# Attention in units of 256 tokens by 4 heads: q and k loaded as token pairs, scores as products of 32 rows

## The chip, the core and the metric

The kernel runs on one core of one Trainium2 chip. A core has five engines with a queue of instructions each: TensorE (PE in the profile; the loads of its stationary operand are shown as PEld), VectorE (DVE), ScalarE (ACT), GpSimd (POOL) and SyncE (SP), which here only issues DMAs. Sixteen DMA engines move data between HBM and the on-chip memory SBUF. TensorE writes its results to PSUM, which has 128 partitions and eight banks of 512 float32 values per partition. The metric is the device time of one execution in microseconds (us); lower is better.

## The reference

Inputs are q, k and v of shape 8 x 8 x 576 x 64 (batch, heads, tokens, head width) and two weight matrices, `w_in` (512 x 2048) and `w_out` (2048 x 512), all float32. What is computed, cut to its core:

```python
# attention within chunks of 64 tokens, 9 chunks per batch and head
scores = q_c @ k_c.T / 8
attn = exp(scores - max(scores)); attn /= sum(attn) + 1e-9
out = attn @ v_c
x = out.transpose(0, 2, 1, 3).reshape(4608, 512)   # 8 heads side by side
h = x @ w_in
g = softplus(h)
return g @ w_out                                   # 4608 x 512
```

## The kernel before

**The matrix products.** The 4608 rows of x are treated in nine groups of 512. Each group needs a first product with `w_in` (lines 632 to 642, and line 777 for the six last groups, which are taken in pairs and use a scheme with seven products in place of eight), a softplus, and a second product with `w_out` (line 831). Both run in the format fp32r; each value is split into a high and a low part, so each product consists of three terms. Almost all of TensorE's time goes into these.

**The attention.** A block is 128 rows of x: two chunks of 64 tokens, all 8 heads. There are 36 blocks, four per group of rows. The first four blocks are computed at the start, with TensorE doing the transposes (lines 384 to 450): `pe_t` transposes q and k through PSUM, `pe_tq` and `pe_tk` copy them out on ScalarE, `pe_s` makes the scores, `pe_e` transposes the exponentials, `pe_v` multiplies by v. The other 32 blocks (lines 470 to 609) are worked off between the matrix products: VectorE transposes q and k in 32 x 32 squares (`blk_t`), `blk_s` makes the scores on TensorE, VectorE takes the maximum and subtracts it, ScalarE the exponential, and after the division VectorE transposes the exponentials (`blk_e4`; for four blocks `blk_swap` with DMAs), and `blk_v` multiplies by v.

On TensorE `blk_s` and `blk_v` of two blocks stand together in what the code calls a burst (line 624): v of one pair of blocks and scores of the next pair, in the order v, scores, v, scores. A product there is float32, 64 x 64 x 64, and takes one of four quarters of the array (two halves of the rows by two halves of the columns). `blk_s` and `blk_v` issue 16 such products per block; `pe_s` also 16, but on two quarters alone. There are 17 bursts: the first has scores only, the last v only.

**The loads.** For 32 x 32 transposes on VectorE to turn a 64 x 64 piece into its transpose, its four squares must already lie in exchanged places. For most blocks eight DMAs of 32 KB per tensor put them there (lines 479 to 489), each row of a square being a packet of 128 bytes. Blocks 4, 5 and 9 (`WHOLE`) and the first four are loaded in one or two DMAs with packets of 256 bytes (one token, one head); for blocks 4, 5 and 9 VectorE then moves the squares with four extra transposes of 32 partitions (`blk_t4`). v comes in four DMAs per block.

**The order.** All engines' instructions are written out by a planner (class `Plan`): each task has an engine, an assumed cost, its needs, an urgency and the buffers that it takes. The planner runs through its own clock and emits the tasks in the order in which they would start; so each engine's queue has a fixed order, and an instruction that waits holds up all behind it on its engine. The sequence of the matrix products and bursts on TensorE is fixed by a list (`seq`). The tiles `pa` (two of two PSUM banks each) hold the first product's results, and those of the bursts; the tiles `po` (four of one bank) hold the second product's.

Of the kernel before, what the change touches and what calls it, by code (L numbers as in the profile page):

```python
# [33 lines left out]
class Plan:  # L34
# [10 lines left out]
    HOLD_FROM = 120.0  # L45

# [4 lines left out]
    def add(  # L51
        self, name, eng, cost, fn, needs=(), urg=0.0, table=None, take=(), kb=0, slack=0.0, after=(), port=False, parts=1,
        late={}, room={}
    ):
        self.tasks[name] = dict(
            name=name, eng=eng, cost=cost, fn=fn, needs=list(needs) + list(after), after=set(after), urg=urg, table=table,
            take=take, kb=kb, slack=slack, seq=len(self.tasks), port=port or eng == "POOL", parts=parts, late=late, room=room,
        )
# [97 lines left out]
def chunked_attention_softplus_ffn(  # L156
# [9 lines left out]
    nc = tc.nc  # L166
# [3 lines left out]
    C = 64  # L170
# [172 lines left out]
    def hd(t):  # L343
        return t.rearrange("p (h d) -> p h d", d=D)

    def rows_of(i):
        b, c = divmod(2 * i, NCH)
        if c + 1 < NCH:
            return [(0, P, b, c * C)]
        return [(0, C, b, c * C), (C, C, b + 1, 0)]  # L350

    def pe_load(eng, i, src, n):
        dst = hd(slot(i, n))
        for p0, rows, b, s0 in rows_of(i):
            eng.dma_start(  # L355
                dst[p0 : p0 + rows], src[b, :, s0 : s0 + rows, :].rearrange("h s d -> s h d")
            )
# [3 lines left out]

    def v_load(i, t):
        dv = t.rearrange("p (j c d) -> p j c d", c=2, d=D)
        for c2 in range(2):
            b, c = divmod(2 * i + c2, NCH)
            for a in range(2):
                loader("v", i).dma_start(
                    dv[a * C : (a + 1) * C, :, c2, :],
                    v[b, a * HP : (a + 1) * HP, c * C : (c + 1) * C, :].rearrange("h s d -> s h d"),
                )  # L370
        live["v", i] = t.rearrange("p (j d) -> p j d", d=D)
# [12 lines left out]
    def pe_t(i):  # L384
        if i < 2:
            tq, tk = (po_tile(n) for n in range(2))
        else:
            pa = pa_tile()
            tq, tk = pa[:, 0, :], pa[:, 1, :]
        keep_warm(tq)  # L390
        for dst, n in ((tq, 0), (tk, 1)):
            src = hd(slot(i, n))
            for hp in range(HP):
                nc.tensor.transpose(
                    dst[:, hp * P : (hp + 1) * P], src[:, 2 * hp : 2 * hp + 2, :], ident
                )
        live["t", i] = tq, tk

    def pe_tq(i):
        nc.scalar.copy(slot(i, 3), live["t", i][0])  # L400

    def pe_tk(i):
        copy = nc.scalar.copy if i not in TK else nc.vector.tensor_copy
        copy(slot(i, 4), live["t", i][1])

    def pe_s(i):
        qT, kT = (slot(i, n).rearrange("p (a t) -> p a t", a=HP) for n in (3, 4))
        sc = po_tile(2 + i % 2)
        keep_warm(sc)
        for hp in range(HP):  # L410
            for c2 in range(2):
                for h2 in range(2):
                    r = slice(h2 * C, (h2 + 1) * C)
                    t = slice(c2 * C, (c2 + 1) * C)
                    col = (2 * hp + c2) * C
                    nc.tensor.matmul(
                        sc[r, col : col + C], qT[r, hp, t], kT[r, hp, t], start=hp + c2 == 0, stop=True,
                        skip_group_check=True,
                    )
        live["sc", i] = sc.rearrange("p (a c k) -> p a c k", c=2, k=C)  # L420
        live["e", i] = slot(i, 0).rearrange("p (a c k) -> p a c k", c=2, k=C)

    def pe_e(i):
        tp = po_tile(i)
        keep_warm(tp)
        for hp in range(HP):
            nc.tensor.transpose(tp[:, hp * P : (hp + 1) * P], live["e", i][:, hp], ident)
        live["et", i] = tp
# [4 lines left out]
    def pe_v(i):  # L433
        eT, vt = slot(i, 1).rearrange("p (a t) -> p a t", a=HP), hd(slot(i, 2))
        pa = pa_tile()
        xp = [pa[:, 0, :], pa[:, 1, :]]
        keep_warm(xp[0])
        for hp in range(HP):
            for h2 in range(2):
                for c2 in range(2):  # L440
                    o = slice(((h2 + c2) % 2) * C, ((h2 + c2) % 2 + 1) * C)
                    r = slice(c2 * C, (c2 + 1) * C)
                    nc.tensor.matmul(
                        xp[c2][o, hp * C : (hp + 1) * C],
                        vt[r, 2 * hp + (h2 + c2) % 2, :],
                        eT[r, hp, o],
                        start=True,
                        stop=True,
                    )
        live["xp", i] = pa[:, :, : HP * C].rearrange("p c (a t) -> p c a t", t=C)  # L450
# [19 lines left out]
    def blk_load(i, name, src):  # L470
        dst = home(name, i)
        live[name, i] = dst
        if i in WHOLE:
            for p0, rows, b, s0 in rows_of(i):
                loader(name, i).dma_start(
# [869 lines left out]
```

## Time and profile before

| | |
|---|---|
| time, median of 3 runs | 833.47 us (832.66 to 834.87) |
| the profiled execution's own time | 831.63 us |
| its span, first to last instruction | 829.2 us |
| TensorE busy | 817.2 us, 99% |
| VectorE, ScalarE, GpSimd busy | 487.7, 381.5, 327.0 us |
| DMA packets | 189512, of which 152704 under 512 bytes |
| granted TensorE clock | 0.999 |

The page says how long each engine was busy. "PE" counts the time in which a product was under way, so it hides the small steps between products, and the start of the next piece must be compared with the start of the one before. A float32 product leaves two records, so 16 products show as x32. In a timeline row the columns are start, duration, engine, line, operation, output and inputs, shape, count, and in square brackets how long the engine had been idle before and what ended that. The chain of waits goes back from the last instruction to whatever released each step.

### The profile page before, as it was taken

The page shows a single profiled execution, that of the slowest core. Times are in us where ns is not written, and L with a number is a line of the kernel's source. Part 1 is how long each engine was busy: PE and PEld are TensorE (multiplying, and loading weights), DVE is VectorE, ACT ScalarE, POOL GpSimd, SP SyncE. Part 2 cuts the span into 40 slices and gives each one's busy share as a digit, 9 for nine tenths or more (in the row PEclk, how much of TensorE's full clock was granted, in tenths as well). Part 3 has the DMA queues.
Part 4 walks back from the last instruction along what each step waited for, and adds up shares of the span by engine and source line. Part 5 has one row for each costly group of instructions (what it writes and reads, how often), then busy time and mean ns, then how long its engine had stood idle before and what let it go on. Part 6 is the DMA issues. An engine that isn't in the chain of part 4 may idle for free.

```text
span 829.2 us, 15241 instructions
## 1 busy us (share of the span) xinstructions
PE 817.2 (99%) x5745; PEld 671.5 (81%) x5745; DVE 487.7 (59%) x769; ACT 381.5 (46%) x612; POOL 327.0 (39%) x380
## 2 busy tenths in 40 slices
PE   9899999999999999999999999999999999999998
PEld 7787888888888888888887878888888888888886
DVE  3988985367556587374677786573866632232322
ACT  4867765444534473353543543443444343333322
POOL 1655569686987753212224411222230021321100
PEclk9999999999999999999999999999999999999999
DMA  9987757754475446876576427678362165354322
GB/s 205 268 215 178 212 153 225 218 151 113 84 188 127 115 151 205 211 211 173 161 221 179 127 104 230 172 199 229 120 215 78 51 219 175 117 187 153 102 102 76
DMA packets 189512, 137.33 MB, mean 166 GB/s; under 512 B 152704, under 2 KB 166272, under 8 KB 186496
## 3 DMA queue, kind: packets, MB, share of 16 engines
q1 hardware_dynamic: 178400, 86.68, 38.6%
q0 software_dynamic: 10896, 49.56, 19.4%
q8 instruction: 45, 0.74, 0.4%
q14 instruction: 27, 0.22, 0.1%
q10 hardware_dynamic: 144, 0.13, 0.0%
HBM read 100.14 MB, written 35.13 MB: 163 GB/s over the span
## 4 chain that ended last, share of the span: by engine, by line
PE 91%; DMA 3%; SPq 2%; DVE 2%; ACT 1%; issue 0%; POOL 0%; DVEq 0%; POOLq 0%
PE po L831 46%; PE pa L777 27%; PE pa L641 14%; PE pa L605 2%; SPq L355 2%; PE pa L517 2%; DMA raw<-in_moe_w_out_dram 1%; DMA q<-in_q_dram 1%; DMA raw<-in_moe_w_in_dram 1%; DVE wib L767 0%; SPq L269 0%; DVE mx L562 0%; DMA out_dram<-raw 0%; POOL wib L328 0%; DVE wib L328 0%
## 5 line engine op out<-in xcount | busy, mean ns | idle before, releaser
L796 POOL TENSOR_TENSOR wib<-wib 128x512 f32<-128x512 f32 x48 | 63.5, 1323 | 275.6 <-ACT wib L783 273.7
L831 PE MATMUL po<-late,g_hi 128*128 128x512 f32 x538 | 165.8, 391 | 0.0
L657 DVE TENSOR_TENSOR g_lo<-ends,g_hi 128x512 fp32r<-128x512 f32 x96 | 66.3, 691 | 98.3 <-ACT g_hi L653 94.7
L831 PEld LDWEIGHTS po<-late,g_hi 128*128 128x128 f32 x538 | 100.3, 188 | 21.3 <-DVE late L328 0.3
L777 PE MATMUL pa<-wi_hi,xb 128*128 128x512 f32 x368 | 113.3, 389 | 0.0
L653 ACT CAST g_hi<-ends 128x512 fp32r<-128x512 f32 x96 | 59.3, 618 | 114.7 <-PE po L831 111.3
L831 PE MATMUL po<-wo_hi,g_hi 128*128 128x512 f32 x288 | 109.7, 393 | 0.0
L831 PE MATMUL po<-wo_lo,g_hi 128*128 128x512 f32 x288 | 108.7, 390 | 0.6 <-POOL wo_lo L328 0.6
L831 PE MATMUL po<-late,g_lo 128*128 128x512 f32 x287 | 108.0, 390 | 0.7 <-issue 0.7
L831 PE MATMUL po<-wo_hi,g_lo 128*128 128x512 f32 x288 | 108.5, 389 | 0.0
L777 PE MATMUL pa<-wib,xb 128*128 128x512 f32 x432 | 104.2, 394 | 0.7 <-DVE wib L767 0.7
L777 PEld LDWEIGHTS pa<-wib,xb 128*128 128x128 f32 x432 | 79.2, 188 | 21.8 <-ACT wib L783 5.4
L796 DVE TENSOR_TENSOR wib<-wib,pa 128x512 f32<-128x512 f32 x72 | 49.6, 689 | 66.1 <-PE pa L777 51.4
L777 PEld LDWEIGHTS pa<-wi_hi,xb 128*128 128x128 f32 x368 | 69.0, 188 | 14.4
L777 PE MATMUL pa<-wi_lo,xb 128*128 128x512 f32 x184 | 71.6, 389 | 0.0
L649 ACT ACTIVATE u<-pa 128x512 f32<-128x512 f32 (+1 forms) x50 | 29.1, 581 | 89.0 <-PE pa L641 85.9
L783 ACT COPY wib<-pa 128x512 f32<-128x512 f32 x72 | 39.9, 589 | 62.3 <-PE pa L777 62.3
L804 ACT ACTIVATE ends<-pa 128x512 f32<-128x512 f32 x48 | 28.7, 599 | 80.5 <-PE pa L777 55.7
L831 PEld LDWEIGHTS po<-late,g_lo 128*128 128x128 f32 x287 | 53.9, 188 | 12.4 <-issue 1.1
L831 PEld LDWEIGHTS po<-wo_lo,g_hi 128*128 128x128 f32 x288 | 54.0, 188 | 12.1 <-POOL wo_lo L328 1.1
L831 PEld LDWEIGHTS po<-wo_hi,g_lo 128*128 128x128 f32 x288 | 54.1, 188 | 11.3
L831 PEld LDWEIGHTS po<-wo_hi,g_hi 128*128 128x128 f32 x288 | 53.7, 188 | 11.5 <-POOL wo_hi L324 0.2
(189 smaller groups left out, 1368.9 us busy)
## 6 DMA issues: line engine op xcount, KB each, us to landing
xb<-scratch POOLq DMA_DIRECT2D x23, 1024.0 KB, 5.6
xb<-scratch POOLq DMA_DIRECT2D x24, 768.0 KB, 7.4
spill<-ends SPq DMA_DIRECT2D x21, 512.0 KB, 6.8
ends<-spill SPq DMA_DIRECT2D x21, 512.0 KB, 3.3
out_dram<-raw SPq DMA_DIRECT2D x35, 256.0 KB, 2.8
raw<-in_moe_w_in_dram SPq DMA_DIRECT2D x16, 512.0 KB, 5.6
raw<-in_moe_w_out_dram SPq DMA_DIRECT2D x16, 512.0 KB, 4.4
scratch<-ends SPq DMA_DIRECT2D x16, 512.0 KB, 3.2
```

Of the source, the lines that this page charges most:

```text
L355: eng.dma_start(dst[p0 : p0 + rows], src[b, :, s0 : s0 + rows, :].rearrange("h s d -> s h d"))
L517: nc.tensor.matmul(pa[o, c2, col : col + C], qT[r, a * HP + hl, :], kT[r, a * HP + hl, :], start=True, stop=True,)
L605: nc.tensor.matmul(pa[o, a, col : col + C], vt[r, 4 * j + 2 * h2 + c2, :], eT[r, :, 4 * c2 + 2 * j + h2, :], start=True, stop=True,)
L641: nc.tensor.matmul(ph, wt[:, c, :], x[:, ts_, c, :], start=(n == 0), stop=(n == 3 * KC - 1))
L649: nc.scalar.activation(w["u"], w["ph"], AF.Softplus)
L653: nc.scalar.copy(w["hi"], w["u"])
L657: (nc.gpsimd if pool else nc.vector).tensor_tensor(w["lo"], w["u"], w["hi"].bitcast(F32), op=ALU.subtract)
L777: nc.tensor.matmul(w["bank"][BANK[k]], wts[:, q, c, :], x[:, c, :], start=k < NX and c + n == 0, stop=c == 1 and n == 2, skip_group_check= ...
L783: nc.scalar.copy(tmp_of(n), w["bank"][n])
L796: (nc.gpsimd if what in MIX_POOL else nc.vector).tensor_tensor(out, a, b, op=op)
L804: nc.scalar.activation(u_tiles(j)[i], src, AF.Softplus)
L831: nc.tensor.matmul(pos[w["m"]][t], terms[n][0][:, j * P : (j + 1) * P], terms[n][1], start=(w["first"] and n == 0), stop=n == 2 and (w["la ...
```

## The change

The unit of the attention becomes 256 tokens (four chunks) by 4 heads, in place of 128 tokens by 8 heads. It still has 128 partitions by 512 values, and there are still 36, four for each group of 512 rows.

- **Loads of q and k.** A partition gets a pair of tokens of a chunk, 2 x 64 values that lie side by side in HBM, so a packet has 512 bytes. A unit is one DMA, or two where it reaches into the next batch. v keeps packets of 256 bytes and comes in two DMAs (three at some batch ends).
- **The turn.** One VectorE transpose of 32 x 32 squares (`qk_turn`) now leaves the head width in two halves of 32, each on the 32 partitions of its chunk. It serves the first four units too, where TensorE's transposes and ScalarE's copies (`pe_t`, `pe_tq`, `pe_tk`) go, and takes the place of the extra transposes of `blk_t4`.
- **The scores.** As the head width now lies in two halves on the same 32 partitions, a score is a sum of two products of 32 rows (`a` = 0 and 1): 32 products per unit, on spots of 32 rows by 64 columns of the array; four spots are used, one for each chunk. The second operand is read in steps: its tokens lie as all first ones of the pairs and then all second ones, and reading alternates between the two (distance 32 values). The transposed exponentials are read in the same alternating way in `pe_v` (distance 32 values) and `blk_v` (distance 256 values).
- **The first four units** take their score tiles from `pa` in place of `po`, and `pe_sub` is issued once per bank.
- **The planner** gets new costs for the tasks above (also for `blk_e4`, which has the same instructions as before). The cost of a burst is as it was. A table `SHIFT` of corrections to urgencies is added and left empty.

The diff, cut to what bears on the order and the engines:

```diff
+    def unit(src, i, first, count):
+        at = i // 2 * 4 + first
+        b, c = divmod(at, NCH)
+        n = min(count, NCH - c)
+        yield first, n, src[b, i % 2 * HP : (i % 2 + 1) * HP, c * C : (c + n) * C, :]
+        if n < count:
+            yield from unit(src, i, first + n, count - n)
...
+    def qk_load(eng, i, src, dst):
+        for c, n, rows in unit(src, i, 0, 4):
+            eng.dma_start(
+                dst[c * BL : (c + n) * BL].rearrange("p (h e) -> p h e", h=HP), rows.rearrange("h (p t) d -> p h (t d)", t=2)
+            )
...
+    def qk_turn(dst, src):
+        nc.vector.transpose(dst.rearrange("p (a x e) -> p x a e", a=2, e=BL), src.rearrange("p (x a e) -> p x a e", a=2, e=BL))
...
-                nc.tensor.transpose(
-                    dst[:, hp * P : (hp + 1) * P], src[:, 2 * hp : 2 * hp + 2, :], ident
-                )
-        live["t", i] = tq, tk
-
-    def pe_tq(i):
-        nc.scalar.copy(slot(i, 3), live["t", i][0])
...
+    def pe_t(i, n):
+        qk_turn(slot(i, 3 + n), slot(i, n))
+
+    def scores(sc, q_, k_, cy, cz):
+        qT, kT = (t.rearrange("p (a h t) -> p a h t", a=2, h=HP) for t in (q_, k_))
+        for h in range(HP):
+            for a in range(2):
+                for z in range(2):
+                    for y in range(2):
+                        r = slice((cz * z + cy * y) * BL, (cz * z + cy * y + 1) * BL)
+                        nc.tensor.matmul(
+                            sc[y * C : (y + 1) * C, z, h * C : (h + 1) * C], qT[r, a, h],
+                            kT[r, a, h].rearrange("p (t g) -> p g t", t=2),
+                            start=h + a == 0, stop=True, skip_group_check=True,
+                        )
+        return sc.rearrange("p z (h k) -> p z h k", h=HP)
...
     def blk_s(i, pa):
         e, ea = live.pop(("qT", i)), live.pop(("kT", i))
-        qT, kT = (t.rearrange("p (h t) -> p h t", h=H) for t in (e, ea))
-        for hl in range(HP):
-            for a in range(2):
-                for c2 in range(2):
-                    r = slice(c2 * C, (c2 + 1) * C)
-                    o = slice(a * C, (a + 1) * C)
-                    col = (hl // 2) * 2 * P + P + (hl % 2) * C
-                    nc.tensor.matmul(
-                        pa[o, c2, col : col + C], qT[r, a * HP + hl, :], kT[r, a * HP + hl, :],
-                        start=True, stop=True,
-                    )
...
+        live["sc", i] = scores(pa[:, :, HP * C :], e, ea, 1, 2)
...
     def blk_v(i, pa):
...
-                            pa[o, a, col : col + C], vt[r, 4 * j + 2 * h2 + c2, :], eT[r, :, 4 * c2 + 2 * j + h2, :],
+                            pa[h % 2 * C : (h % 2 + 1) * C, y, col : col + C], vt[r, z, h, :],
+                            eT[r, :, 2 * h + z, :].rearrange("p t g -> p g t"),
...
-    WHOLE = (4, 5, 9)
...
-        plan.add(f"T{i}", "PE", 1.0, partial(pe_t, i), [f"q{i}", f"k{i}"], urg=d,
-                 take=[("po0", [f"tq{i}"]), ("po1", [f"tk{i}"])] if i < 2 else [("pa", [f"tq{i}", f"tk{i}"])])
-        plan.add(f"tq{i}", "ACT", 0.58, partial(pe_tq, i), [f"T{i}"], urg=d + 1 * kw)
-        plan.add(f"tk{i}", "DVE" if i in TK else "ACT", 0.60, partial(pe_tk, i), [f"T{i}"], urg=d + 1 * kw)
+        for pl, n in enumerate("qk"):
+            plan.add(f"t{n}{i}", "DVE", 0.7, partial(pe_t, i, pl), [f"{n}{i}"], urg=d + 1 * kw)
...
-                plan.add(f"{n}{i}", LOADER.get((n, i), "SP"), 0.55 * two if whole else 4.6, partial(blk_load, i, n, src), free_of[n, i],
-                         urg=d - QK_URG, kb=310 if whole else 430, parts=two if whole else 8,
-                         after=[QK_AFTER if ps == F else K6_AFTER])
+                plan.add(f"{n}{i}", LOADER.get((n, i), "SP"), 0.6 * pieces(i, 0), partial(blk_load, i, n, src), free_of[n, i],
+                         urg=d - QK_URG, kb=270, parts=pieces(i, 0), after=[QK_AFTER if ps == F else K6_AFTER])
```

How the instructions stand now, in three places. First TensorE at the second burst, which stands behind a first product (`pa` from the x tile `xb`) and ahead of a second one (`po`). Before:

```order
L641 MATMUL pa<-xb,wib 128x512 x12
L605 MATMUL pa<-eT,xa 64x64 x16
L517 MATMUL pa<-ka,qe 64x64 x16
L605 MATMUL pa<-eT,xa 64x64 x16
L517 MATMUL pa<-ka,qe 64x64 x16
L831 MATMUL po_495<-wo_hi,g_hi 128x512
```

Now (lines 593, 557, 403 and 783 are the former 641, 605, 517 and 831):

```order
L593 MATMUL pa<-xb,wib 128x512 x12
L557 MATMUL pa<-eT,xa 64x64 x16
L403 MATMUL pa<-ka,qe 64x64 x32
L557 MATMUL pa<-eT,xa 64x64 x16
L403 MATMUL pa<-ka,qe 64x64 x32
L783 MATMUL po_531<-wo_hi,g_hi 128x512
```

The same bursts stand at the same places of the sequence; each group of score products (`ka` and `qe` are the turned k and q) has 32 instructions where it had 16. Behind the start the other products on TensorE follow each other as before, but for two warming products (line 384).

Second SyncE's queue behind the v loads of the first four blocks, where weights (`raw`) and q and k of blocks 4 and 5 are loaded. Before:

```order
L274 DMA raw_252<-in_moe_w_out_dram 128x2048
L269 DMA raw_261<-in_moe_w_in_dram 128x4x512
L269 DMA raw_306<-in_moe_w_in_dram 128x4x512
L475 DMA q<-in_q_dram 64x8x64 x2
L475 DMA k<-in_k_dram 64x8x64 x2
L274 DMA raw_380<-in_moe_w_out_dram 128x2048
L475 DMA xa<-in_q_dram 128x8x64
L269 DMA raw_418<-in_moe_w_in_dram 128x4x512
L475 DMA xa<-in_k_dram 128x8x64
```

Now:

```order
L276 DMA raw_323<-in_moe_w_out_dram 128x2048
L271 DMA raw_327<-in_moe_w_in_dram 128x4x512
L271 DMA raw_339<-in_moe_w_in_dram 128x4x512
L359 DMA q<-in_q_dram 32x4x128
L359 DMA q<-in_q_dram 96x4x128
L359 DMA k<-in_k_dram 32x4x128
L359 DMA k<-in_k_dram 96x4x128
L359 DMA xa<-in_q_dram 32x4x128
L359 DMA xa<-in_q_dram 96x4x128
L359 DMA xa<-in_k_dram 32x4x128
L359 DMA xa<-in_k_dram 96x4x128
L276 DMA raw_497<-in_moe_w_out_dram 128x2048
```

The loads of block 5 (into the x tile `xa`) moved ahead of the second `w_out` load, and the row length of a packet went from 64 to 128 values.

Third VectorE's queue at the very start. Before, from its first instruction of the attention:

```order
L562 TENSOR_REDUCE mx<-po_165 128x8
L585 TENSOR_REDUCE den<-late 128x8
L586 TENSOR_SCALAR den<-den 128x8
L587 RECIPROCAL den<-den 128x8
L562 TENSOR_REDUCE mx<-po_213 128x8
```

Now:

```order
L371 STREAM_TRANSPOSE late<-late 128x8x2x32 x4
L515 TENSOR_REDUCE mx<-pa 128x8
L371 STREAM_TRANSPOSE qe<-xa 128x8x2x32
L371 STREAM_TRANSPOSE ka<-xa 128x8x2x32
L515 TENSOR_REDUCE mx<-pa 128x8
L371 STREAM_TRANSPOSE late<-late 128x8x2x32 x2
L537 TENSOR_REDUCE den<-late 128x8
```

The turns of q and k of the first four units (`late` and `xa` hold them) stand between the maxima (`mx`) and the sums (`den`) of the softmax; two turns stand ahead of the second unit's maximum, and two more ahead of the first sum.

More of the change, by code (lines that the diff above doesn't have):

```diff
@@ L55, in add @@
         self.tasks[name] = dict(
-            name=name, eng=eng, cost=cost, fn=fn, needs=list(needs) + list(after), after=set(after), urg=urg, table=table,
+            name=name, eng=eng, cost=cost, fn=fn, needs=list(needs) + list(after), after=set(after), table=table,
+            urg=urg + self.SHIFT.get(name, 0.0),
             take=take, kb=kb, slack=slack, seq=len(self.tasks), port=port or eng == "POOL", parts=parts, late=late, room=room,
@@ new lines, in pieces, with v_load @@
+    def pieces(i, n):
+        steps = (4,) if n < 2 else (2, 2)
+        return sum(1 for j, c in enumerate(steps) for _ in unit(q, i, j * c, c))
+    def qk_load(eng, i, src, dst):
[3 more added lines that the diff above has]
+            )
+    def v_load(eng, i, dst):
+        dst = dst.rearrange("p (z h d) -> p z h d", z=2, h=HP)
+        for z in range(2):
+            for c, n, rows in unit(v, i, 2 * z, 2):
+                y = c - 2 * z
+                eng.dma_start(dst[y * C : (y + n) * C, z], rows.rearrange("h p d -> p h d"))
@@ L423, in pe_e @@
+    def pe_s(i):
+        sc = pa_tile()[:, :, : HP * C]
+        keep_warm(sc[:, 0])
+        live["sc", i] = scores(sc, slot(i, 3), slot(i, 4), 2, 1)
+        live["e", i] = slot(i, 0).rearrange("p (h z k) -> p z h k", z=2, h=HP)
     def pe_e(i):
-        tp = po_tile(i)
+        tp = po_tile(2 + i % 2)
         keep_warm(tp)
-        for hp in range(HP):
-            nc.tensor.transpose(tp[:, hp * P : (hp + 1) * P], live["e", i][:, hp], ident)
+        for n in range(HP):
+            nc.tensor.transpose(tp[:, n * P : (n + 1) * P], slot(i, 0)[:, n * P : (n + 1) * P], ident)
@@ L527, in blk_e @@
     def blk_e(i):
[L528 to L529 removed]
+        live.pop(("e", i))
+        nc.vector.transpose(live["eA", i], live.pop(("eS", i)))
     def blk_et(i):
@@ L572, in pe_sub @@
         sc, mx = live["sc", i], live.pop(("mx", i))
-        nc.tensor.matmul(
-            sc, minus, mx.unsqueeze(3).to_broadcast(list(sc.shape)), start=False, stop=True,
-            skip_group_check=True,
-        )
+        mx = mx.unsqueeze(3).to_broadcast(list(sc.shape))
+        for c in range(2):
+            nc.tensor.matmul(sc[:, c], minus, mx[:, c], start=False, stop=True, skip_group_check=True)
     def att_exp(i):
```

187 lines of the change are left out of this document (52 added, 135 removed).

## The prediction

> **What bounds the kernel now.** I read the page first (busy times, then the chain of waits), then the table of stretches, to see where TensorE has any idle time left.
>
> ```profile
> span 829.2 us, 15241 instructions
> PE 817.2 (99%) x5745; PEld 671.5 (81%) x5745; DVE 487.7 (59%) x769; ACT 381.5 (46%) x612; POOL 327.0 (39%) x380
> PE 91%; DMA 3%; SPq 2%; DVE 2%; ACT 1%; issue 0%; POOL 0%; DVEq 0%; POOLq 0%
> ```
>
> ```profile
> core 0: us, PE busy (x) PEld busy (x) DVE busy (x) ACT busy (x) POOL busy (x), PEclk, DMA share, GB/s
> 0.00:20.00 20.00, 18.03 (x211) 15.47 (x212) 7.24 (x13) 8.37 (x15) 3.04 (x9) 1.00 1.00 199
> 20.00:41.50 21.50, 18.08 (x222) 14.81 (x221) 19.65 (x36) 18.27 (x34) 14.43 (x16) 1.00 1.03 272
> 41.50:83.00 41.50, 40.05 (x349) 32.27 (x348) 35.06 (x57) 28.80 (x48) 21.32 (x20) 1.00 0.79 196
> 83.00:330.00 247.00, 247.00 (x1912) 203.91 (x1913) 165.00 (x264) 127.62 (x198) 175.88 (x199) 1.00 0.59 163
> 330.00:829.00 499.00, 494.06 (x3056) 405.00 (x3054) 260.77 (x403) 198.46 (x321) 112.34 (x138) 1.00 0.53 159
> ```
>
> TensorE is busy 99% of the span and carries 91% of the chain. Between 83 and 330 us it is busy 247.00 of 247.00 us; in the last stretch 4.94 us are idle, the wait for the last store among them. So what is added to TensorE's own work behind the start comes out at the end almost whole, and what is taken from any other engine, or from the DMA engines (0.53 to 0.59 of their time there), is worth nothing. Only ahead of some 41 us is TensorE not the bound: the DMA engines are full (1.00, 1.03), and TensorE partly does warming products (line 375).
>
> **The scores, the largest term.** A burst in the timeline and in the chain:
>
> ```profile
> 118.07 0.61 PE L641 MATMUL pa<-xb,wib 128*128 128x512 f32 x2
> 118.61 0.69 PE L605 MATMUL pa<-eT,q 64*64 64x64 f32 x32
> 119.13 0.65 PE L517 MATMUL pa<-ka,qe 64*64 64x64 f32 x32
> 119.59 0.65 PE L605 MATMUL pa<-eT,k 64*64 64x64 f32 x32
> 120.06 0.65 PE L517 MATMUL pa<-ka,qe 64*64 64x64 f32 x32
> 120.64 0.73 PE L831 MATMUL po<-late,g_hi 128*128 128x512 f32 x2
> ```
>
> ```profile
> 115.96 2.72 PE pa L641 x12
> 118.68 0.62 PE pa L605 x32
> 119.31 0.47 PE pa L517 x32
> 119.77 0.47 PE pa L605 x32
> 120.24 0.47 PE pa L517 x32
> 120.71 2.95 PE po L831 x12
> ```
>
> The 16 score products of one block take 0.46 to 0.47 us from start to next start. How does that depend on how many of them run at once? The start of the program has the same products on two quarters of the array alone:
>
> ```profile
> 15.66 1.15 PE L416 MATMUL po<-late 64*64 64x64 f32 x32
> 16.64 1.10 PE L416 MATMUL po<-ka,qe 64*64 64x64 f32 x32
> ```
>
> There 16 products take 16.64 - 15.66 = 0.98 us, twice as long: the same work on half of the spots. So a round, one product on each spot in use, costs about 0.117 us (0.467 / 4 rounds of four; 0.98 / 8 rounds of two gives 0.122), and the number of spots decides how many rounds there are. The change has 32 products on four spots: 8 rounds, 0.93 us. That a product has 32 rows in place of 64 saves nothing by this reading, as a round streams 64 columns in either case. It adds 0.467 us per unit. The number of units behind the start:
>
> ```profile
> L517 PE MATMUL pa<-ka,qe 64*64 64x64 f32 x1024 | 21.0, 219 | 0.7 <-DVE ka L493 0.6
> ```
>
> 1024 records at 32 per block are 32 blocks: 32 x 0.467 = **14.9 us**, all on the path. At the start `pe_s` has 8 rounds in either version and gets no dearer.
>
> **The switches inside a burst.** Now v uses spots of 64 rows and the scores spots of 32, so the array's division changes between them. The only such switches in the trace are those between the full array and quarters, in and out of a burst. From the chain: the burst takes 120.71 - 118.68 = 2.03 us, its four groups 4 x 0.467 = 1.87; 0.16 are lost, and the group of 12 full products behind it takes 2.95 in place of 2.72, so 0.39 for the two switches. A full burst (v, scores, v, scores) gets three new ones; the first of the 17 bursts has scores alone and the last v alone, which leaves 15 x 3 = 45. The bounds are 0 (no switch cost between two small divisions) and 0.20 each (half of 0.39), 0 to 9.0 us. I take 0.15: the 0.23 behind the burst is the full product's own late start, and the 0.16 is what small products pay. 45 x 0.15 = **6.8 us**. [...]
>
> **The start.** q and k of blocks 0 to 5 go from packets of 256 to 512 bytes. Twelve loads of 0.262 MB are 3.15 MB, 15.8 us at the 199 GB/s of the first stretch. At the 272 GB/s of the second, which has more of the long weight rows at the same full DMA engines, they would take 11.6. So up to 4.2 us come out of the start if all of it waits for the DMA engines. It does in part:
>
> ```profile
> 19.13 7.69 DMA q<-in_q_dram
> 26.91 0.72 DVE qe L501
> 28.57 0.83 DVE wi_lo L328
> 30.15 1.67 PE pa L641 x12
> ```
>
> The chain reaches the second first product (30.15) through block 4's q. On the other side VectorE now turns q and k of the first four units; its queue runs in order, and two turns stand ahead of the second unit's maximum. A turn is taken from the same transpose of later blocks:
>
> ```profile
> L493 DVE STREAM_TRANSPOSE qe<-q 128x512 f32<-128x512 f32 x16 | 11.4, 710 | 4.3 <-DMA q<-in_q_dram 3.9
> L504 DVE STREAM_TRANSPOSE qe<-q 32x256 f32<-32x256 f32 x8 | 3.5, 436 | 0.2
> ```
>
> Two of 0.71 are 1.4 us of possible loss: the start is worth -4.2 to +1.4. I take **-2.5 us**, nearer to the gain, since the DMA engines are full and ScalarE's eight copies and TensorE's transposes go too, but not all of it, since v and the weights load as before.
>
> **Costed at nothing.** Eight DMAs of 32 KB per q or k become one or two, and with it several us of SyncE's and GpSimd's issue time; the extra transposes of blocks 4, 5 and 9 (such as the second row above) go. All of it lies beside TensorE's unbroken work behind 41 us. If that cover were gone, the gain there would still be no more than the 1.45 us idle between 41.5 and 83 (41.50 - 40.05). The new views of the maximum, the exponential and the copy to x have the same 128 x 512 values. The planner still assumes the old burst; on TensorE the burst stands where it stood, and a longer burst gives the engines behind it more time, not less.
>
> **Sum.** The profiled execution took 831.63 us (829.2 of it the span). 831.63 + 14.9 + 6.8 - 2.5 = 850.8. The median of the runs is 833.47, 1.84 above that execution, so **852.7 us**. With the ends of the terms: 833.47 + 14.9 + (0 to 9.0) + (-4.2 to 1.4) is 844 to 859.
>
> **Rivals.**
>
> *Reading in steps is slow (chance 0.24).* The second operands of the scores and of v now jump 32 or 256 values from each element to the next. No product of the trace reads so. The nearest rows are ScalarE's, where L292 reads every second 4-byte value and L282 every fourth 2-byte one, beside a plain copy of the same size:
>
> ```profile
> L292 ACT ACTIVATE wib<-raw 128x512 int32<-128x512 uint32 x15 | 10.1, 671 | 0.1
> L282 ACT CAST ends<-raw 128x512 f16<-128x512 bf16 x23 | 18.0, 784 | 3.6 <-DMA raw<-in_moe_w_in_dram 2.4 <-DMA raw<-in_moe_w_out_dram 0.6 <-DVE ends L297 0.5
> L653 ACT CAST g_hi<-ends 128x512 fp32r<-128x512 f32 x96 | 59.3, 618 | 114.7 <-PE po L831 111.3 <-DVE eT L538 2.1 <-issue 1.2
> ```
>
> They are 9% and 27% dearer than 618 ns. The scores and v of a unit are 0.93 + 0.47 = 1.40 us, 44.8 us over 32 units; 9 to 27% of it are 4 to 12 us, and if each jump cost as much again as the element, 44.8. That gives 857 to 897 us. Against it: the small products take their columns slowly. A round of 0.117 us serves two records of 64 columns, 0.91 ns a column, while the 12 products of 512 columns in 2.72 us take 0.44 ns a column, so the reading of a float32 product has slack of a factor two to hide a jump in. [...]
>
> *Spots in one bank (chance 0.04).* Two of the four spots now write to the same PSUM bank, in different halves of the partitions. If they took turns, the scores would double once more: 32 x 0.93 = 29.8, 882 us. Against it speaks L416 above, whose two quarters also write halves of one bank, and whose 0.98 us would be twice as long if they took turns.
>
> *Not slower (chance 0.08).* If TensorE ran both halves of the sum at once, on the half of the array that the four spots leave free, the scores would stay at 0.467 us. The switches then cost nothing if they need no wait, and the start gives its full 4.2: 833.47 - 4.2 = 829.3 us, faster. It decides below an addition of 2.5 / 32 = 0.08 us per unit, switches included. Against it: both halves of one score sit on the same spot, as they lie on the same 32 partitions, and L416 shows that a spot's next product waits a full round.
>
> **Chances.** The forecast has 0.64. About 0.3% (2.5 us) is what a measurement of this kernel can tell from no change. Faster by more 0.05, within it 0.03 (both from the last rival), slower 0.92. The likeliest case alone spans 844 to 859. For 8 in 10 I go up into the first two rivals, to 890; below 844 (0.08) and a full doubling of the reads (0.11) are left out.
>
> **What will show it.** Right: a group of 32 score products takes 0.93 us from its start to the next group's, v still 0.47, and 0.1 to 0.2 more at each change from v to scores and back; TensorE again without a pause behind 41 us; the first pair of full products some 2 to 3 us earlier than 30.15. The reads in steps would show in v groups longer than 0.47, the turns in one bank in score groups of 1.9, the last rival in score groups of 0.47. The forecast is wrong above all if TensorE gets pauses behind bursts, where a first product waits for `pa` to be freed by a late subtraction or copy. Before, that happened once, for 0.70 us, and I expect no more:
>
> ```profile
> 82.88 0.93 PE L641 MATMUL pa<-xb,wib 128*128 128x512 f32 x3 [0.70 <-DVE qe L567]
> ```

## The result and the profile after

The changed kernel takes 883.34 us, median of 4 runs (881.23 to 886.28); the kernel before, run beside it, 833.07. The ratio is 1.060, 95% interval 1.056 to 1.064: 50 us slower, where 19 were forecast, and within the forecast range (844 to 890). The profiled execution took 884.67 us. First the page, then the table of stretches (columns as before: busy time and records of each engine, granted clock, DMA share, GB/s):

```profile
span 882.9 us, 16805 instructions
PE 857.3 (97%) x6881; PEld 705.1 (80%) x6881; DVE 482.3 (55%) x753; ACT 375.4 (43%) x604; POOL 275.9 (31%) x295
```

```profile
20.00:41.50 21.50, 17.36 (x178) 14.50 (x170) 15.33 (x22) 14.85 (x28) 10.60 (x13) 0.92 0.88 257
83.00:330.00 247.00, 241.19 (x2278) 199.14 (x2279) 137.04 (x224) 116.18 (x180) 134.19 (x135) 0.99 0.45 143
330.00:882.90 552.90, 540.66 (x3622) 442.68 (x3620) 282.73 (x437) 209.91 (x343) 104.59 (x117) 0.99 0.46 152
```

TensorE is still the bound, with 40 us more work, but now it also has idle time (5.8 us between 83 and 330, where it had none; 0.9 of it is a wait for a weight tile, the rest the pauses below) and its granted clock is no longer 1.00 throughout. The engines beside it and the DMA engines have less to do than before (GpSimd 275.9 us for 327.0, DMA share 0.45 for 0.59 between 83 and 330 us), which is worth nothing, as forecast.

A burst without a pause, in the chain of waits (start, duration, engine, output, line, records):

```profile
172.19 0.71 PE pa L557 x32
172.91 1.26 PE pa L403 x64
174.17 0.85 PE pa L557 x32
175.02 1.26 PE pa L403 x64
```

v groups take 0.71 us, score groups 1.26 (medians over all bursts by the records' starts: 0.711 and 1.263; the 0.85 of the second v group here is not typical). Inside a group four records, half a round, take 69.5 ns, where they took 58 before; and each change between v and scores adds 0.15 us. And a burst with a pause, in the timeline:

```profile
81.25 1.04 PE L403 MATMUL pa<-ka,qe 32*64 32x64 f32 x45
85.07 0.90 PE L403 MATMUL pa<-ka,qe 32*64 32x64 f32 x19 [2.78 <-issue]
85.90 2.08 PE L783 MATMUL po<-wo_hi,g_hi 128*128 128x512 f32 x4
87.77 1.91 PE L783 MATMUL po<-wo_lo,g_hi 128*128 128x512 f32 x4
```

TensorE stops in the middle of a score group for 2.78 us, and "issue" says that it waits for nothing that the profile shows: no engine, no DMA, no buffer. Behind the pause four products of 512 columns take 1.87 us from start to start in place of 0.91: the clock is at half. The view of waits sums the pauses in score groups (total, times, longest), and the stretch behind this one has its clock in the last but two columns:

```profile
PE pa L403 <- issue: 12.5, 8, 3.3
PE po L783 <- issue: 1.0, 1, 1.0
```

```profile
84.20:91.04 6.84, 5.97 (x31) 0.50 0.55 159
```

Half clock of 6.8 us follows each of the three pauses of about 3 us (at 82, 382 and 437 us), some 2.5 us lost each.

**Where the pauses stand.** The DMA view counts the packets of instructions of TensorE's queue; before, then after:

```profile
q8 instruction: 45, 0.74, 0.4%
```

```profile
q8 instruction: 54, 0.88, 0.4%
```

Each has 16 KB. Counting TensorE's instructions in the trace (products, loads of the stationary operand, waits), the eight pauses come behind instruction 1986, 2754, 4034, 5314, 5826, 7362, 8129 and 9410. Modulo 256 that is 194 seven times and 193 once; the single pause at line 783 (behind 11202) is 194 too. The stretches from the start to the first and to the second pause show it without the waits:

```profile
0.00:82.50 82.50, 75.48 (x983) 63.26 (x983) 62.07 (x93) 49.27 (x82) 36.59 (x43) 0.98 0.76 217
0.00:132.50 132.50, 121.75 (x1362) 101.14 (x1362) 94.33 (x140) 78.38 (x129) 60.86 (x67) 0.96 0.69 195
```

2 x (1362 - 983) = 758 products and loads lie between, with 10 waits 768 = 3 x 256. And 54 packets x 256 are 13,824 of the 13,896 instructions counted. So a packet holds 256 instructions (an "instruction page" below), and TensorE stops at the boundaries between these pages. A float32 product has four instructions (two products and two loads in the trace): a full burst had 64 products, 256 instructions, as many as one instruction page, and now has 96, 384 instructions. An instruction page that lies wholly in a burst is used up in 2.6 us (256 of 384 instructions in 3.95 us), among products of 512 columns in some 29 (128 products by 0.227 us).

### The profile page after: what moved, and what is told of

It reads as the page before. It is cut to its first block, busy times and chain, and to the rows that moved or that the text cites. A ratio compares the mean times of both kernels' runs of the same rounds, so it can differ in the third digit from the quotient of the medians.

```text
span 882.9 us, 16805 instructions
## 1 busy us (share of the span) xinstructions
PE 857.3 (97%) x6881; PEld 705.1 (80%) x6881; DVE 482.3 (55%) x753; ACT 375.4 (43%) x604; POOL 275.9 (31%) x295
## 4 chain that ended last, share of the span: by engine, by line
PE 93%; DVE 2%; issue 2%; DMA 1%; ACT 1%; POOL 0%; SPq 0%; DVEq 0%; POOLq 0%; ACTq 0%
PE po L783 44%; PE pa L729 26%; PE pa L593 14%; PE pa L403 5%; PE pa L557 3%; PE pa L384 1%; DMA k<-in_k_dram 1%; DMA raw<-in_moe_w_out_dram 0%; DVE mx L515 0%; DVE wib L719 0%; DMA out_dram<-raw 0%; DVE den L537 0%; DVE ends L299 0%; ACT wib L294 0%; POOL wo_lo L330 0%
## 5 line engine op out<-in xcount | busy, mean ns | idle before, releaser
L783 PE MATMUL po<-wo_hi,g_hi 128*128 128x512 f32 x288 | 111.7, 401 | 1.3 <-POOL wo_hi L326 1.3
L783 PE MATMUL po<-wo_lo,g_hi 128*128 128x512 f32 x288 | 111.0, 398 | 1.0 <-POOL wo_lo L330 1.0
L783 PE MATMUL po<-wo_hi,g_lo 128*128 128x512 f32 x288 | 110.7, 397 | 0.0
L756 ACT ACTIVATE ends<-pa 128x512 f32<-128x512 f32 x48 | 26.9, 597 | 79.0 <-DVE wib L748 75.9
```

Of the source, the lines that this page charges most:

```text
L756: nc.scalar.activation(u_tiles(j)[i], src, AF.Softplus)
L783: nc.tensor.matmul(pos[w["m"]][t], terms[n][0][:, j * P : (j + 1) * P], terms[n][1], start=(w["first"] and n == 0), stop=n == 2 and (w["la ...
```

## The experiments

**1. Plain reads.**

```diff
-    kT[r, a, h].rearrange("p (t g) -> p g t", t=2),
+    kT[r, a, h],
-    eT[r, :, 2 * h + z, :].rearrange("p t g -> p g t"),
+    eF[r, (2 * h + z) * C : (2 * h + z + 1) * C],     # the same in pe_v
```

> Changed: the second operands of the score products and of the v products are read one value after another, as before the change, and not in steps. The keys and tokens then come in another order, so the output is not the reference's; the instructions, their number and their order are those of the changed kernel. Theory (reading in steps slows a round): the half-rounds of the small products go from 69.5 ns back to 58.3, scores and v alike; 24 half-rounds x 11.2 ns x 32 units = 8.6 us less work on TensorE. Theory on the pauses (a run of 256 TensorE instructions that lies wholly in a burst is through before the next 16 KB of instructions are there): in the eight bursts with a pause the pause grows by what the reads save between the two boundaries, so only about (7 + 8/3)/15 of it is seen, 5.5 us: 878 us, 874 to 881. Rival (the slow rounds come from the spots of 32 rows or from the supply of instructions): half-rounds stay at 69 ns, 883 us.

880.9 us, ratio 1.057 (1.055 to 1.059). The half-rounds are back at 58 ns in scores and v, so the reads in steps do cost 19% (chain):

```profile
173.47 1.09 PE pa L403 x64
174.56 0.66 PE pa L558 x32
```

But only 2.4 us of 8.6 come out (3.6 between the profiled executions), less than expected. The pauses sit at the same eight places and have grown by more than I allowed for, from 12.5 to 15.7 us, and the one at the second product (line 784 here) from 1.0 to 1.8; about 1 us more was not traced:

```profile
PE pa L403 <- issue: 15.7, 8, 4.1
```

**2. Half of the score products.**

```diff
-            for a in range(2):
+            for a in range(1):
```

> Left out: the second of the two products of which each score is the sum (a = 1), so the scores are half sums and the output is not the reference's. 16 products of 32 rows per unit remain; a full burst has 256 TensorE instructions again, in place of 384. Theory (instruction pages): a run of 256 instructions between two page boundaries no longer fits into a burst but for rare luck, so the pauses of 0.4 to 3.3 us in the score groups and the half clock behind the long ones go: 883.3 - 32 x 0.556 (8 half-rounds of 69.5 ns) - 12.5 - 7.5 = 845.5 us, 843 to 849. Rival (the pauses belong to score products on spots of 32 rows, or to the engines around the burst): pauses stay in some bursts, 860 to 866 us.

845.6 us, ratio 1.015 (1.013 to 1.016), as the theory of instruction pages had it. No wait on "issue" in any score group. This kernel has the 32-row spots, the steps and the switches, but 256 instructions per burst.

**3. The kernel before with its score products twice.**

```diff
-        for hl in range(HP):
+        for hl in [hl for hl in range(HP) for _ in range(2)]:
```

> The kernel before, with each score product of the 32 later blocks issued twice over (64 rows, four quarters, no reading in steps, no change of the array's division inside a burst; the second writes the same values). A full burst has 384 TensorE instructions, as after the change. Theory (instruction pages): 833.1 + 14.9 for the doubled rounds, plus pauses in those bursts whose first instruction stands at most 128 ahead of a page boundary. Counted from the trace of before with 128 more per burst these are 9 of the 15 full bursts, the 1st, 2nd, 4th, 6th, 7th, 9th, 10th, 12th and 14th; a page takes 1.9 us of plain rounds, and the shortest times between two boundaries seen were 3.2 to 6.1, so 1.3 to 4 us each, and half clock behind some: 860 to 885 us, likeliest 869. Rival (pauses come from the spots of 32 rows or from summing two products): no pauses, 848 us, 846 to 850.

881.9 us, ratio 1.058 (1.054 to 1.063): as much as the whole loss, with nothing of the change but the number of products. That the two times are so near each other is chance: this kernel has no reading in steps and no inner switches, but twice the pauses (21.2 + 6.3 us). Groups of 64 records take 0.933 us (16 half-rounds of 58.3 ns), so the doubled rounds are worth the 14.9 us of the forecast; the rest is pauses.

```profile
L517 PE MATMUL pa<-ka,qe 64*64 64x64 f32 x2048 | 38.7, 221 | 21.4 <-issue 21.2
```

```profile
373.62 0.63 PE L517 MATMUL pa<-ka,qe 64*64 64x64 f32 x29
378.99 1.16 PE L517 MATMUL pa<-ka,qe 64*64 64x64 f32 x35 [4.74 <-issue]
```

Of the nine bursts named, seven pause in their scores for 1.65 us or more, the 12th for 0.15, the 7th not. Three more pauses (behind the 3rd, the 11th and the 13th burst) stand at line 831, again at place 193 or 194 modulo 256, where an instruction page ends just behind a burst. The pauses are longer than I expected (up to 4.74), since plain rounds use an instruction page up in 1.9 us.

**4. 128 more instructions ahead of everything.**

```diff
+        for _ in range(32 if i == 0 else 0):
+            nc.tensor.matmul(sc[:BL, 0, :BL], ident[:BL, :BL], ident[:BL, :BL], start=True, stop=True)
         keep_warm(sc[:, 0])
```

> The changed kernel with 32 small extra products (32 x 32 x 32 of the identity, 128 TensorE instructions) ahead of the first warming products, where TensorE has nothing to do; all else as it is. Theory (instruction pages): every later instruction stands 128 places further on against the page boundaries. The eight bursts that paused (those at 78.6, 128.2, 198.2, 262.0, 288.7, 378.4, 434.0, 505.5 us) pause no more, and the other seven do (172.1, 230.6, 315.3, 474.2, 572.9, 622.3, 657.9 us): the pauses move, the time stays within some us, 875 to 892. Rival (the pauses depend on what the other engines, the loads or the spots do in those bursts): the same eight bursts pause, 883 to 885 us.

875.3 us, ratio 1.050 (1.048 to 1.052), though the extra products hold the start up by 4 us. None of the eight bursts pauses any more; four of the seven named do, at their new time:

```profile
PE pa L403 <- issue: 5.8, 4, 3.4
```

```profile
85.06 1.33 PE L403 MATMUL pa<-ka,qe 32*64 32x64 f32 x64
...
560.50 0.50 PE L403 MATMUL pa<-ka,qe 32*64 32x64 f32 x16
564.35 1.56 PE L403 MATMUL pa<-ka,qe 32*64 32x64 f32 x48 [3.35 <-issue]
```

The first row is the group that had paused for 2.78 us. The rival falls: the data, the loads and the other engines' tasks of a burst are the same, its place in the stream of instructions has changed.

**5. Half sums and plain reads.** Experiments 1 and 2 together.

> The kernel with half sums (second product of each score left out) and in addition the plain reads: no steps in the second operands of scores and v. Neither the number nor the order of instructions differs from that kernel, whose time was 845.6 us without a pause in a burst; the output is not the reference's in either. Theory (steps cost 11 ns per half-round wherever nothing else eats the gain): 16 half-rounds x 11.2 ns x 32 units = 5.7 us less, 839.9 us, 838.5 to 841. What is left above the kernel before (833.6) is then the 45 switches of the array's division, 6.8 by their 0.15 us each, and the start. Rival (the steps only move time into some wait): 844 to 846.

839.0 us, ratio 1.008 (1.006 to 1.009). Where no pause eats it, the whole 5.7 us (here 6.6) come out. What is left is 6.2 us above the kernel before, with rounds, instructions and reading like before: mainly the switches, and the start. In the chain a burst reads 0.62, 0.64, 0.62 where the kernel before had 0.47 for the last three groups:

```profile
162.08 0.62 PE pa L403 x32
162.70 0.64 PE pa L558 x32
163.34 0.62 PE pa L403 x32
```

**6. The start: q and k of unit 5 behind the second load of w_out.**

```diff
-     after=[QK_AFTER if ps == F else K6_AFTER])
+     after=["load4" if i == 5 else QK_AFTER if ps == F else K6_AFTER])
```

> The kernel with half sums (845.6 us, output not the reference's), and q and k of unit 5 loaded behind the second load of w_out, where the kernel before had them; steps and switches stay. Theory (the start's gain was lost because that w_out load was issued 3.5 us later): it lands some 3 us earlier, TensorE no longer waits 1.2 and 0.6 us for GpSimd's wo_hi and wo_lo at 33.7 and 35.6 us, and the half clock behind goes: 2 to 3 us less, 843 us. Rival (the first products are bound by the weights' decoding on ScalarE and GpSimd or by the DMA engines as a whole): 845 to 846, the waits only get another name.

847.3 us, ratio 1.017 (1.015 to 1.018), not faster than experiment 2. My theory falls: the load is issued at 27.73 us, no earlier than in the changed kernel (27.12), though it stands ahead now, because its buffer comes free only when ScalarE has decoded the weights that lay in it (line 294, from 26.97 us). GpSimd's second wo_hi comes no earlier either.

```profile
26.97 0.69 ACT L294 ACTIVATE wib<-raw 128x512 int32<-128x512 uint32 x1
27.73 0.35 SPq L276 DMA_DIRECT2D raw<-in_moe_w_out_dram  x1
...
34.57 0.61 POOL L326 CAST wo_hi<-wib 128x512 fp32r<-128x512 f32 x1 [0.61 <-DVE wib L299]
```

**7. A second product between the halves of the first eight full bursts.**

```diff
-            seq += [f"B{w['g']}_{j}" for j in range(2) if w["g"] in bursts]
+            seq += [f"B{w['g']}_0"] if w["g"] in bursts else []
         if n >= LAG:
             seq.append(f"G2_{plain[n - LAG]['name']}")
+        if n >= HALVES:
+            seq += [f"B{w['g']}_1"] if w["g"] in bursts else []
```

> The changed kernel with a second product (12 products of 512 columns, 2.7 us) between the two halves of each of the first eight full bursts (78 to 315 us); the last seven are as they were, and the instructions ahead of these are as many as before. The output stays the reference's. Theory (instruction pages): a half burst has 192 TensorE instructions, so no run of 256 lies in it; the five pauses of the first eight bursts (2.78, 1.31, 0.69, 0.37, 0.49 us) and the half clock behind the first go, 5.6 + 2.5 us; an exit and an entry (0.39) take the place of one inner switch (0.15), 8 x 0.24 = 1.9 more; the pauses of the later bursts (3.15, 3.30, 0.41 us) stay where they are. 883.3 - 8.1 + 1.9 = 877 us, 873 to 880. Rival (pauses come from score groups or the spots): the pauses stay, 885 us.

895.2 us, ratio 1.075 (1.072 to 1.077): my number missed by 18 us. The part on instruction pages held: no wait on "issue" in the eight split bursts. But the first of them now meets the wait that I had feared in the prediction, for a subtraction that frees `pa`; and the planner set other numbers of warming products, 45 instructions more, so that two later bursts (573 and 622 us in the changed kernel) came to places 118 and 97 ahead of a boundary and paused, the first for 2.62 us (the four pauses in score groups of this run make 12.4 us):

```profile
85.02 1.33 PE L403 MATMUL pa<-ka,qe 32*64 32x64 f32 x64
89.14 2.26 PE L384 MATMUL pa<-ident 128*128 128x128 f32 x9 [2.78 <-DVE qe L520]
...
581.13 1.31 PE L403 MATMUL pa<-ka,qe 32*64 32x64 f32 x58
585.07 0.36 PE L403 MATMUL pa<-ka,qe 32*64 32x64 f32 x6 [2.62 <-issue]
```

Waits that the changed kernel does not have, for `xb` (3.2 us in three) and `g_lo` (1.4 us in two), are a further part of the miss. The whole of it was not added up.

**8. The kernel before with the changed form in the first four units alone** (`pe_load` to `pe_v`, `pe_sub` and their tasks from the change; all else from before).

> The kernel before, with the changed form for the first four units alone (512-byte loads of q and k, turn on VectorE, no transposes of q and k on TensorE and no copies of them on ScalarE, scores as 32 products of 32 rows); the other 32 blocks, their bursts and their loads are those of before, and the second load of w_out keeps its place ahead of q and k of block 5. The output stays the reference's. Theory (the changed start is worth something when it does not push the weights back): the first products come 2.5 to 2.8 us earlier as in the changed kernel, and some of it stays: 831 us, 830 to 832.5. Rival (the start is bound by the weights): 833 to 834, no change.

848.6 us, ratio 1.019 (1.017 to 1.021). It told nothing of the start: the planner, with new costs at the start, also moved loads further on; k of block 7 was issued at 78.60 us, and TensorE waited 7.47 us for its turn.

```profile
86.94 1.13 PE L525 MATMUL pa<-ka,qe 64*64 64x64 f32 x32 [7.47 <-DVE ka L501]
```

**9. The same with the order of all other tasks held.**

```diff
+        for names in HELD.values():            # each engine's tasks in the order of the kernel before
+            for past, n in zip(names, names[1:]):
+                if past not in T[n]["needs"]:
+                    T[n]["needs"].append(past)
+                    T[n]["after"].add(past)
```

> The kernel before with the changed form for the first four units alone, as in the run before, but now all other tasks keep on each engine the order that they have in the kernel before, so that no load or turn of a later block comes late. The output stays the reference's. Theory (the changed start is worth something by itself, and the run before lost it to a late load of k and to pages): no wait of several us behind 41 us; the first products come 2.5 us earlier, and what the second load of w_out allows of it stays: 831 to 832.5, ratio 0.997 to 0.999. Rival (the start is bound by the weights, whose buffers come free when ScalarE has decoded them): 833, ratio 1.000, the gain is gone by the third product.

832.3 us, ratio 0.9997 (0.9988 to 1.0005): no change. The first products come 2.6 us earlier (22.18 for 24.76 us), and the gain is gone at GpSimd's second wo_hi, which starts at 34.09 us here, at 34.01 in the kernel before and at 33.97 in the changed one:

```profile
34.09 0.61 POOL L338 CAST wo_hi<-wib 128x512 fp32r<-128x512 f32 x1 [1.02 <-DVE wib L311]
```

```profile
34.01 0.61 POOL L324 CAST wo_hi<-wib 128x512 fp32r<-128x512 f32 x1 [1.02 <-ACT wib L292]
```

So here the weights bound the start. Which of their steps does was not taken apart.

**10. One switch fewer in each burst** (second half: scores ahead of v; base is experiment 5).

```diff
-        if p_v is not None:
+        if p_v is not None and n == 0:
             blk_v(2 * p_v + n, pa)
         if p_s is not None:
             blk_s(2 * p_s + n, pa)
+        if p_v is not None and n == 1:
+            blk_v(2 * p_v + n, pa)
```

> The kernel with half sums and plain reads (839.0 us, output not the reference's), with the second half of each burst turned round: v, scores, scores, v in place of v, scores, v, scores. Same products, one inner change of the array's division less in each of the 15 full bursts. Theory (each change costs 0.158 us on TensorE, as the groups of 0.625 against 0.467 us show): 15 x 0.158 = 2.4 us less, 836.6 us. Rival (a change costs nothing by itself, the longer groups come from something else, as the supply of instructions): 839.

836.2 us, ratio 1.004 (1.003 to 1.006), 2.7 us under experiment 5, forecast 2.4. The two score groups run into each other as one of 64 records in 1.09 us:

```profile
160.11 0.62 PE pa L558 x32
160.73 1.09 PE pa L403 x64
161.82 0.64 PE pa L558 x32
```

**11. Eight ways of reading.**

```diff
+     s, c = ((1, 64), (2, 1), (4, 1), (8, 1), (4, 2), (8, 4), (16, 8), (32, 16))[2 * h + a]
-     kT[r, a, h].rearrange("p (t g) -> p g t", t=2),
+     k_[r, :C] if c == C else k_[r, : C // c * s].rearrange("p (x s) -> p x s", s=s)[:, :, :c],
```

> One look at the round times, no verdict on the whole: the changed kernel with the second operand of the score products read in eight different ways, one for each of the eight rounds of a unit: 64 values side by side; every 2nd, 4th and 8th value; 2 of each 4, 4 of each 8, 8 of each 16 and 16 of each 32 side by side. The output is not the reference's. Theory A (a value costs more as soon as the next one is not its neighbour): 58 ns per half-round for the first way alone, 69 for every 2nd to 8th, less the longer the pieces are. Theory B (only a jump out of a stretch of 16 bytes, four values, costs): every 2nd near 64, 4th and 8th at 69 or more, and pieces of 4 and more values at 58 or little above. Theory C (only jumps as wide as those of the change, 32 and 256 values, cost): 58 for all eight.

The first and the second half-round of each way, by the starts of the records, medians over the 30 units of the full bursts (the first round of a unit is hidden by the switch, the last by what follows):

| every 2nd value | every 4th | every 8th | 2 of 4 | 4 of 8 | 8 of 16 |
|---|---|---|---|---|---|
| 61, 59 ns | 96, 115 | 117, 117 | 78.5, 58 | 56, 58 | 58, 58 |

A first half-round still carries something of the way before it: "2 of 4" comes right behind the slowest way and starts with 78.5, "every 4th" comes behind a fast one and starts with 96. So the second figure is the better one. Theories A and C fall. The figures of theory B hold but for every 2nd value (59 in place of 64); that its 16 bytes are the limit was not shown. The ways of reading that take half of the values or more cost 58 to 59 ns, those that take one of four or of eight 115 to 117. The change's own reading, which takes the values of two places in turn, costs 69.5, and the share of values taken does not explain that.

**12. 188 more instructions, the best place by the count.**

```diff
+        for _ in range(64 if i == 0 else 0):
+            nc.tensor.matmul(sc[:BL, 0, :BL], ident[:BL, :BL], ident[:BL, :BL], start=True, stop=True)
+        if i == 0:
+            plan.gap = 0.0      # no warming products besides
         keep_warm(sc[:, 0])
```

> The changed kernel with the 17 warming products ahead of the first scores cut into 64 small ones (32 x 32 x 32), so that 188 more TensorE instructions stand ahead of all that follows, with little time added. The output stays the reference's. 188 is the number at which, by the count of instructions in the trace of the changed kernel, the fewest full bursts hold a whole page of 256: those at 230.6, 288.7, 315.3 and 657.9 us (places 46, 118, 46 and 67 ahead of a boundary). Theory (instruction pages): no other burst pauses, and of these four not all, as the page is sometimes there in time: 883.3 - 12.5 - 7.5 + 1 to 4 pauses of 0.4 to 3.3 us with some half clock + about 1 at the start = 866 to 874, likeliest 870. Rival (the gain of the run with 128 more instructions was chance): 880 to 886.

867.7 us, ratio 1.043 (1.041 to 1.046): 15.7 us faster than the changed kernel, by a shift in the stream of instructions (and 17 warming products at the start cut into 64 small ones). In score groups exactly the four named bursts pause, 1.6 us together; one more pause, of 1.5 us, stands at line 787 and was not named. No half clock follows behind 41.5 us but the one at the very end (granted clock of the whole run 0.997, of the changed kernel 0.986). The first of the four, and the sums:

```profile
227.32 1.04 PE L403 MATMUL pa<-ka,qe 32*64 32x64 f32 x42 [0.23 <-issue]
```

```profile
PE pa L403 <- issue: 1.6, 4, 0.7
PE po L787 <- issue: 1.5, 1, 1.5
```

No version beats the kernel before: what the change saves (loads, issues, other engines' time) is off the path, and the start's gain does not last.

## Why the prediction was wrong

**The step that failed** is "TensorE again without a pause behind 41 us". The first section's "what is added to TensorE's own work behind the start comes out at the end almost whole" held for the work, but I took it to be all that comes out, and put waits for instructions at nothing without a reason. I counted products by the time that they take and never as instructions that must be fetched. The one warning in the kernel before was a wait that I did not look into, at place 194 modulo 256 as well:

```profile
PE po L831 <- issue: 0.7, 1, 0.7
```

I had named pauses as what would prove me wrong, but behind bursts and for `pa`. They came inside bursts, for instructions: 12.5 us in score groups, 1.0 at line 783, and 7.5 of half clock behind the long ones, 21 us in all. Experiments 2, 3, 4 and 12 show it: taking the instructions away takes the pauses away, adding them to the kernel before brings the pauses there, and shifting the stream moves them to the bursts named beforehand. In the trace the packets have 16 KB, and the pauses stand, to within one instruction, multiples of 256 apart.

**"Reading in steps" was a rival (0.24), and it holds.** It costs 11.2 ns on each of 24 half-rounds of a unit, 24 x 11.2 x 32 = 8.6 us, inside its 4 to 12. My argument against it, a slack of a factor two in the reading of a float32 product, is refuted by experiment 1. Experiment 11 shows where there is slack: a reading that takes two of each four values costs 58 to 59 ns per half-round, no more than a plain one (58.3); one that takes a single value of each four or eight costs 115 to 117.

**That 883 us lies within 844 to 890 is luck.** The range reached beyond 859 for the sake of this rival and of turns in one bank. The rival gave 8.6 us of the distance; the larger part came from pauses, which stood in no term and in no rival.

**The sizes that were right.** The doubled rounds: 0.933 us per group of 64 records, 14.9 us (experiment 3). The switches: 0.158 us each, 45 x 0.158 = 7.1 for 6.8 (experiments 5 and 10), nearer to the choice from rows than to either bound (0 and 9.0). The turns in one bank and both halves at once did not happen: a round of four costs 0.116 us with plain reads, as before.

**The start** was forecast at -2.5 and came out at +1.8. The same first product, in the chain before and after:

```profile
40.05 2.72 PE pa L641 x12
```

```profile
41.86 2.72 PE pa L593 x12
```

The first products do come 2.6 to 2.8 us earlier, but the gain is gone when the second `wo_hi` arrives: the products that wait for it start at 34.63 us (34.68 before), and those for `wo_lo` at 36.33 (36.04). The other 1.5 us come at half clock, from 36.43 to 39.84 us, after TensorE's waits for `wo_hi` and `wo_lo`; the kernel before had its full clock there. Experiment 9 shows that the early products are worth nothing. I had looked for the gain where the chain then ran (q of block 4) and not asked what must arrive next. It is the weights: the second `wo_hi` starts between 33.97 and 34.57 us in the kernels before and after and in experiments 6 and 9. That the load order was to blame was my second error (experiment 6).

**The sum**, by the profiled executions: 14.9 rounds + 7.1 switches + 8.6 reading + 13.5 pauses + 7.5 half clock + 1.8 start = 53.4; the last product of TensorE comes 53.8 us later than before. It is not as exact as it looks. Three waits of 0.65 to 0.70 us of the kernel before are gone and one of 0.89 is new, and a pause reads some 0.3 us shorter than the burst grows by it, as the ends of products are modelled; these are left out, and would together add some 1.5 us.

## What to carry to other kernels

Count the instructions of a run of small products, not only their time: here a boundary inside a run stopped the engine where 256 of TensorE's instructions, with the loads, were used up sooner than the next ones arrived (256 took 2.6 us here without a pause; from boundary to boundary with one it was 3.2 to 6.1 us in the changed kernel, up to 6.9 in experiment 3). A wait on "issue" at a constant place modulo 256 (193 or 194 here) showed it, and 128 or 188 more instructions far ahead moved it (experiments 4 and 12). Splitting each score product in two cost twice, in rounds (14.9 us) and in instructions (384 in a full burst in place of 256). An early start was worth only what the next input to arrive allowed (first products 2.6 us earlier, ratio 0.9997, experiment 9).

## What the runs showed of the hardware

**How late the next instructions come, and what the DMA engines did then.** In every pause that I followed the next packet starts only after the boundary before it has been crossed, and products go on 2.2 to 3.3 us behind the packet's start. What differs is how late the packet starts. From the crossing to the packet's start, in the changed kernel (columns: stretch and its length, TensorE busy and records, clock, DMA share, GB/s):

```profile
79.53:82.02 2.49, 2.49 (x139) 1.00 1.04 325
263.21:263.85 0.64, 0.64 (x52) 1.00 0.12 26
379.37:382.86 3.49, 2.76 (x142) 1.00 0.84 316
506.26:507.00 0.74, 0.74 (x47) 1.00 0.40 161
```

In the two of these stretches with a DMA share of 0.12 and 0.40 the packet comes 0.6 to 0.7 us behind the crossing and the pause is 0.4 us; in the two with 1.04 and 0.84 it comes 2.5 to 3.5 us behind and the pause is about 3. It is no strict rule (at 199 us the packet came 1.03 us behind at a share of 1.01, at 289 us 1.11 us behind at a share of 0.00), and no run changed the DMA load alone. That the packet waits behind other transfers is therefore a reading of the traces, not shown by an experiment. If it does, a mean DMA share of 0.45 did not make the DMA engines harmless.

**A pause can cost more than itself.** The three pauses of about 3 us in the changed kernel were each followed by 6.8 us at half clock, its pauses of 1.31 us and less by none. In the kernel before with doubled products pauses of 1.65, 2.86 and 4.1 to 4.7 us were followed by 3.4 us, but two of 1.67 us by none. The length of a pause alone did not decide it.
